# The small x load moved to the head of SyncE's queue in a gated attention and MLP decode kernel

## Chip, core and metric

The kernel runs on one core of one Trainium2 chip. The metric is device microseconds of one execution, as a median over runs: 133.84 us before (three runs, 133.84 to 133.92). Profiles come from one profiled execution; their times are counted from the first instruction.

## What is computed

One token x of 576 numbers goes through two branches that a gate mixes. Branch A is attention of 32 query heads, two for each of 16 key heads, over the last 4096 rows of a cache of 32768. Branch B is a two-layer MLP with 4608 hidden units. All inputs are bf16.

```python
g = sigmoid((x * gate_w).sum(-1))
# branch A, W = 4096, 32 heads of 128, 16 key heads
q = (x @ wq).reshape(1, 1, 32, 128)
k, v = k_cache[:, :, -W:], v_cache[:, :, -W:]      # each repeated for two query heads
a = softmax(q @ k.T * 128**-0.5) @ v @ wo
# branch B
b = gelu(x @ w1 + b1) @ w2 + b2
out = g * a + (1 - g) * b
```

Nearly everything that is read is used once: keys and values of 16 MB each, w_q and w_o of 4.5 MB each and w_1 and w_2 of 5 MB each.

## The kernel before

All big loads are issued by SyncE, one after the other on one queue, into SBUF tiles of 128 partitions. Keys and values come in four groups of four key heads (`load_k`, `load_v`, 4 MB each, L104) into three rotating buffers; w_q, w_1 and w_o share two others (`load_flat`, L126). SyncE waits before a load whose buffer is still being read. The w_2 blocks (L710) come last, into the buffers of keys and values.

The order at the start is written by hand. `load_flat` loads the first half of w_q in two pieces: a plain block of 2048 columns (512 KB, 128 rows of 4096 bytes) and the rest (1.75 MB); between the two it calls `first_keys`, which issues the first group of keys and the small load of x. Then come the second half of w_q, the second keys, the rows of b_1 (L159), x_row and gw_row (L163 and L164, for the gate) and the third keys. Two small loads of b_2 are issued by ScalarE (L139). Each load signals one of eight completion semaphores that are given out in turn, and a load that gets one for the second time waits for the earlier load on it.

`x9` holds x as 64 rows of nine numbers, 18 bytes each. TensorE's order is by hand too: it first transposes head 0 of the keys (L281, eight times four 128x128 matmuls, evicted at L290 by VectorE and at L292 by ScalarE), then spreads x over 128 partitions by one matmul with `dup` (L432), from which VectorE writes `x2` (L440). Heads 1 to 3 are transposed next, and then 36 matmuls give q (L451), which use `x2` and all of w_q. Scores, softmax, values, the first MLP layer and the gate follow while keys and values arrive. At the end w_o and w_2 are multiplied as they land (L752 and L771), and the output is copied (L787) and stored (L788).

Of the kernel before, what the change touches and what calls it, by code (L numbers as in the profile page):

```python
# [16 lines left out]
def kernel(  # L17
# [15 lines left out]
    nc = tc.nc  # L33
# [24 lines left out]
    NM = 9  # L58
# [53 lines left out]
    def load_k(m):  # L112
        return load_kv(A_k_cache, m, "k_t")
# [25 lines left out]
        nc.scalar.dma_start(out=b2_r[0:1, o], in_=B_b2.rearrange("(o n) -> o n", o=1)[:, o])  # L139

    x9 = const.tile([P // 2, NM], BF16, name="x9")

    def first_keys():
        k_tiles[0] = load_k(0)
        nc.sync.dma_start(out=x9[:], in_=A_x.rearrange("a b (i m) -> (a b i) m", m=NM))

    QP = 2 * NM
    wq_t = [  # L150
        load_flat(wq_flat, 0, QP * QC, "wq_t", (NQ * QC,), first_keys),
        load_flat(wq_flat, QP * QC, QP * QC, "wq_t"),
    ]
# [4 lines left out]
    for o in range(2):  # L158
        nc.sync.dma_start(  # L159
            out=b1_r[o : o + 32 * (NQ - 1) + 1 : 32],  # L160
            in_=B_b1.rearrange("(o t k n) -> o t k n", o=2, t=NQ, k=2)[o],
# [17 lines left out]
        out=row_f[:], in_=ident_f[:, 0 : 32 * (NQ - 1) + 1 : 32], axis=AX.X, op=ALU.add  # L179
# [4 lines left out]
        out=dup[:].rearrange("k (i e) -> k i e", e=2),  # L184
        in_=ident[0 : P // 2, 0 : P // 2].rearrange("k (i e) -> k i e", e=1).to_broadcast(
            [P // 2, P // 2, 2]
        ),
    )
    par = const.tile([P, 2], FP32, name="par")
    for o in range(2):  # L190
        nc.vector.tensor_reduce(
            out=par[:, o : o + 1],
            in_=ident_f[:].rearrange("p (i o) -> p o i", o=2)[:, o, :],
# [7 lines left out]
        out=turn[:].rearrange("p j (h q) -> p j h q", h=OJ),  # L201
        in_=ident[:].rearrange("p (o q j) -> p j o q", o=1, j=OJ).to_broadcast(
            [P, OJ, OJ, P // OJ]
        ),
# [4 lines left out]
        out=m_r[:], in_=ident_f[:].rearrange("p (s r) -> p r s", r=R), axis=AX.X, op=ALU.add  # L209
# [4 lines left out]
    for t in range(TB):  # L214
        nc.vector.tensor_reduce(
            out=m_b[:, t, :, :],
            in_=ident_f[:].rearrange("p (g t b q) -> p t g q b", g=HT, t=TB, q=2)[:, t],
# [4 lines left out]
        out=m_b[:].rearrange("p t g q -> p (t g q)"),  # L222
# [5 lines left out]
        out=own[:], in_=ident_f[:].rearrange("p (i g) -> p g i", g=HT), axis=AX.X, op=ALU.add  # L228
# [3 lines left out]
        out=own_r[:].rearrange("p (g q) -> p g q", q=2),  # L232
        in_=own[:].rearrange("p (g o) -> p g o", o=1).to_broadcast([P, HT, 2]),
# [3 lines left out]
        out=perm[:].rearrange("p (g i) -> p g i", g=HT),  # L237
        in_=ident[:].rearrange("p (i g) -> p g i", g=HT),
# [3 lines left out]
        out=pick[:], in_=ident[:].rearrange("p (g x q) -> p x g q", g=HT, q=2)  # L242
# [4 lines left out]
        out=m_c[:], in_=ident_f[:].rearrange("p (t c r) -> p c t r", c=BC, r=R), axis=AX.XY,  # L247
# [4 lines left out]
        out=m_hl[:], in_=ident_f[:].rearrange("p (h q) -> p h q", h=OJ), axis=AX.X, op=ALU.add  # L252
# [10 lines left out]
        out=half[:], in_=ident_f[:].rearrange("p (e c) -> p e c", e=2), axis=AX.X, op=ALU.add  # L263
# [4 lines left out]
    for dst, src in ((sel, ident), (sel_f, ident_f)):  # L268
        nc.vector.tensor_copy(
            out=dst[:].rearrange("p l (o h) -> p l o h", o=2),  # L270
            in_=src[:].rearrange("p (h l x) -> p l x h", h=2, l=2)[:, :, 0:2, :],
# [176 lines left out]
    for b in range(NM * NQ):  # L448
        m, t = b // NQ, b % NQ
# [22 lines left out]
    for l in range(2):  # L472
        nc.vector.tensor_copy(
            out=qz[:].rearrange("p (t l e) n -> p t l e n", l=2, e=2)[:, :, l, :, QZ : QZ + 2],
            in_=qT[:, :, l, :].rearrange("p (e q) t -> p t e q", q=2),
# [228 lines left out]
    for g in range(NG):  # L704
# [10 lines left out]
        out=ot[:], in0=o_sb[:], scalar=g_t[:, 0:1], in1=r_sums[:], op0=ALU.mult, op1=ALU.mult  # L715
# [3 lines left out]
    for j in range(OJ):  # L719
# [3 lines left out]
        out=ow_m[:],  # L723
# [5 lines left out]
    with nc.allow_low_precision("one of the sixteen summands is not zero"):  # L729
        nc.vector.tensor_reduce(  # L730
            out=ow[:].rearrange("p j o -> p (j o)"), in_=ow_m[:], axis=AX.X, op=ALU.add
# [17 lines left out]
    for n, four in enumerate(blocks):  # L749
# [11 lines left out]
        out=part_s[:], in0=b2_r[:].rearrange("p (k n) -> p k n", k=2), scalar=omg[:, 0:1],  # L761
# [57 lines left out]
```

## Time and profile before

| what | value |
|---|---|
| median of the runs | 133.84 us |
| the profiled execution | 133.86 us, of which its span 132.1 us |
| TensorE busy (matmul) | 91.1 us |
| VectorE busy | 62.7 us |
| ScalarE busy | 50.3 us |
| bytes moved, mean rate over the span | 53.79 MB, 407 GB/s |
| granted TensorE clock, mean | 0.859 |

The span runs from the first instruction to the last; what lies around it is in the time of an execution but in no row of the profile. An engine's busy time is a sum over the span and does not say whether it lies in the way of the end. The rows of the queue of SyncE (SPq) are the instructions that issue a transfer; the transfer itself runs later, on 16 DMA engines that work through one ring each in the order of issue.

### The profile page before, as it was taken

To read this page: it belongs to the slowest core of one execution; us is meant where nothing else is said; L and a number is where in the kernel's file an instruction comes from. 1 tells how busy PE (TensorE), PEld (TensorE's weight loads), DVE (VectorE), ACT (ScalarE), POOL (GpSimd) and SP (SyncE) were. 2 spreads that over 40 slices of the span, in tenths; PEclk is the share of its full clock that TensorE was granted. 3 is DMA by queue.
4 is the path that set the end of the run, shared out by engine and by line. 5 is a ranking of instruction groups with operands and counts; after the bars stand their busy time and mean duration, and the time that the engine had idled before them with its cause. 6 is when DMAs were issued, how large, how long until landed. Compare 5 with 4: busy or idle time off the path is not lost.

```text
span 132.1 us, 2606 instructions
## 1 busy us (share of the span) xinstructions
PE 91.1 (69%) x1127; PEld 59.6 (45%) x1127; DVE 62.7 (47%) x138; ACT 50.3 (38%) x89; POOL 2.9 (2%) x10
## 2 busy tenths in 40 slices
PE   0000587986498879487899998994799856294761
PEld 0000585653266646256665575761396421252230
DVE  2940356642256546847545457477376262610021
ACT  3000358870177777483465646670600000000001
POOL 8000000000000000000000000000000000000000
PEclk9999999999999999965579999999985555959555
DMA  4999999999999899999989989998999999999970
GB/s 100 535 397 397 413 445 423 466 471 389 409 476 452 367 447 417 406 458 466 447 371 421 473 372 457 466 432 377 457 466 392 424 396 430 430 427 407 434 272 5
DMA packets 3449, 53.79 MB, mean 407 GB/s; under 512 B 483, under 2 KB 750, under 8 KB 1390
## 3 DMA queue, kind: packets, MB, share of 16 engines
q1 hardware_dynamic: 3434, 53.62, 95.5%
q8 instruction: 9, 0.15, 0.4%
q14 instruction: 2, 0.02, 0.0%
q10 hardware_dynamic: 4, 0.00, 0.0%
HBM read 53.62 MB, written 0.00 MB: 406 GB/s over the span
## 4 chain that ended last, share of the span: by engine, by line
DMA 44%; PE 26%; DVE 14%; issue 6%; ACT 5%; SPq 3%; DVEq 0%; ACTq 0%
DMA w_t<-in_B_w_dram 22%; DMA k_t<-in_A_k_cache_dram 21%; PE tp L281 12%; DVE kT L290 6%; PE s_ps L311 4%; ACT kT L292 3%; PE acc L398 3%; PE h_ps L495 2%; PE pT L367 2%; DVE ez L374 2%; ACT pr L355 2%; PE y_ps L771 1%; SPq L126 1%; DVE h_r L514 1%; DVE mx L331 1%
## 5 line engine op out<-in xcount | busy, mean ns | idle before, releaser
L281 PE MATMUL tp<-perm,k_t 128*128 128x128 bf16 x512 | 44.4, 234 | 20.8 <-DMA k_t<-in_A_k_cache_dram 15.9
L292 ACT CAST kT<-tp 128x512 bf16<-128x512 f32 x80 | 44.0, 587 | 38.8 <-PE tp L281 37.2
L281 PEld LDWEIGHTS <-k_t 128*128 128x128 bf16 x512 | 34.5, 105 | 32.1 <-DMA k_t<-in_A_k_cache_dram 16.4
L290 DVE CAST kT<-tp 128x512 bf16<-128x512 f32 x48 | 32.6, 689 | 34.6 <-PE tp L281 30.6
L311 PE MATMUL s_ps<-kT,qz 128*32 128x512 bf16 x128 | 12.6, 409 | 1.2 <-DVE kT L290 0.9
L398 PE MATMUL acc<-v_t,ez 128*32 128x512 bf16 x128 | 13.0, 507 | 0.0
L787 ACT CAST y<-y_ps 1x144 bf16<-1x144 f32 x2 | 0.5, 270 | 27.3 <-PE y_ps L771 27.3
L374 DVE TENSOR_TENSOR ez<-pT,own_r 128x512 bf16<-128x512 f32 x8 | 5.5, 690 | 3.5 <-PE pT L367 3.3
L752 PE MATMUL part<-w_t,gt 128*1 128x288 bf16 x54 | 4.3, 381 | 3.0 <-DMA w_t<-in_B_w_dram 2.8
L760 DVE SCALAR_TENSOR_TENSOR part_s<-b_r,omg,part 128x576 f32<-128x576 bf16 x1 | 0.8, 815 | 10.7 <-PE part L752 10.7
L355 ACT ACTIVATE pr<-ms,nb 128x2048 bf16<-128x2048 f32 x2 | 4.0, 2002 | 4.6 <-DVE nb L352 4.6
L311 PEld LDWEIGHTS <-qz 128*32 128x32 bf16 x128 | 3.6, 94 | 4.6 <-DVE kT L290 1.2
L367 PE MATMUL pT<-pick,pr 128*128 128x128 bf16 x32 | 4.1, 271 | 2.1 <-ACT pr L355 1.1
L398 PEld LDWEIGHTS <-ez 128*32 128x32 bf16 x128 | 3.4, 114 | 3.7 <-issue 2.7
L367 PEld LDWEIGHTS <-pr 128*128 128x128 bf16 x32 | 3.4, 140 | 3.6 <-ACT pr L355 2.1
L526 PE MATMUL hT<-sel_f,h_r 128*128 128x8 f32 x18 | 4.9, 377 | 0.0
L526 PEld LDWEIGHTS hT<-sel_f,h_r 128*128 128x128 f32 x18 | 4.7, 331 | 0.4 <-DVE nb L352 0.4
L752 PE MATMUL part<-wo_t,ow 128*1 128x288 bf16 x64 | 3.6, 407 | 1.5 <-DVE ow L730 1.5
L414 DVE SCALAR_TENSOR_TENSOR a_s<-acc,m_c,a_s 128x128 f32<-128x128 f32 x12 | 4.2, 351 | 0.4
L421 PEld LDWEIGHTS o_ps<-m_r,a_s 128*128 128x128 f32 x8 | 1.6, 250 | 6.2 <-DVE a_s L414 5.3
L421 PE MATMUL o_ps<-m_r,a_s 128*128 128x8 f32 x8 | 2.0, 319 | 3.2 <-DVE a_s L414 3.1
L752 PEld LDWEIGHTS <-gt 128*1 128x1 bf16 x54 | 1.8, 92 | 5.2 <-issue 4.2
(87 smaller groups left out, 46.3 us busy)
## 6 DMA issues: line engine op xcount, KB each, us to landing
k_t<-in_A_k_cache_dram SPq DMA_DIRECT2D x4, 4096.0 KB, 30.3
v_t<-in_A_v_cache_dram SPq DMA_DIRECT2D x4, 4096.0 KB, 26.0
w_t<-in_B_w_dram SPq DMA_DIRECT2D x2, 2592.0 KB
wo_t<-in_A_wo_dram SPq DMA_DIRECT2D x2, 2304.0 KB, 23.9
w_t<-in_B_w_dram SPq DMA_DIRECT2D x2, 1296.0 KB, 27.3
wq_t<-in_A_wq_dram SPq DMA_DIRECT2D x1, 2304.0 KB
wq_t<-in_A_wq_dram SPq DMA_DIRECT2D x1, 1792.0 KB, 16.0
w_t<-in_B_w_dram SPq DMA_DIRECT2D x1, 864.0 KB
```

The costliest lines, as they stand in the source:

```text
L281: nc.tensor.matmul(tp[:, c * P : (c + 1) * P], lhsT=k_tiles[h // UT][:, (h % UT) * NCH + i * BC + c, :], rhs=perm[:], start=True, stop=True,)
L290: nc.vector.tensor_copy(out=dst, in_=tp[:])
L292: nc.scalar.copy(out=dst, in_=tp[:])
L311: nc.tensor.matmul(s_tiles[t // TB][32 * g : 32 * (g + 1), :, :], lhsT=qz[:, HT * t + g, lo : lo + 32], rhs=kT_v[:, s * CB : (s + 1) * CB, ...
L355: nc.scalar.activation(out=pr[:].rearrange("p c i g -> p (c i) g"), in_=ms[:].rearrange("p c (i g) -> p (c i) g", g=1).to_broadcast([P, CB ...
L367: nc.tensor.matmul(pT[:, c, :, :].rearrange("p x r -> p (x r)"), lhsT=pr[:, n * BC + c, :, :].rearrange("p i g -> p (i g)"), rhs=pick[:].r ...
L374: nc.vector.tensor_tensor(out=ez[:, :, :, n, :, :].rearrange("p t b c r -> p c (t b) r"), in0=pT[:], in1=own_r[:].rearrange("p (a b r) -> ...
L398: nc.tensor.matmul(acc[t][32 * ct : 32 * ct + BC * R, :, :], lhsT=ez[:, t % TB, n // NN, n % NN, :, :].rearrange("p c r -> p (c r)"), rhs= ...
L414: nc.vector.scalar_tensor_tensor(out=a_s[:], in0=acc[t][:, c, :], scalar=m_c[:, c : c + 1], in1=a_s[:], op0=ALU.mult, op1=ALU.add,)
L421: nc.tensor.matmul(o_ps[:], lhsT=a_s[:], rhs=m_r[:], start=True, stop=True)
L526: nc.tensor.matmul(box[0][:, j, :, :].rearrange("p e g -> p (e g)"), lhsT=rows[:, j : j + RJ * (P - 1) + 1 : RJ], rhs=sel_f[:].rearrange(" ...
L752: nc.tensor.matmul(part[32 * t : 32 * t + 1, k, 0:DB], lhsT=col, rhs=w[:, i * D + k * DB : i * D + (k + 1) * DB], start=(n == 0), stop=(n ...
```

## The change

The one instruction that loads `x9` is taken out of `first_keys` and stands right behind the allocation of its tile, so that it is issued before `load_flat` is called for the first time. Shape, source and destination stay as they are.

```diff
     x9 = const.tile([P // 2, NM], BF16, name="x9")
+    nc.sync.dma_start(out=x9[:], in_=A_x.rearrange("a b (i m) -> (a b i) m", m=NM))
 
     def first_keys():
         k_tiles[0] = load_k(0)
-        nc.sync.dma_start(out=x9[:], in_=A_x.rearrange("a b (i m) -> (a b i) m", m=NM))
```

SyncE's first transfers are then x, the plain block of w_q, the first keys and the rest of w_q; before, they were the block, the keys, x and the rest. The instructions of the other engines keep their order. The completion semaphores are given out in the order of the program, so the loads at the start get other ones than before.

## The prediction

> **What bounds the kernel now.** I read the slices of the page first, then the table by stretches, then SyncE's own timeline, then the place where x is used.
>
> The page's slices, whose DMA row is the mean busy share of the 16 DMA engines:
>
> ```profile
> span 132.1 us, 2606 instructions
> ...
> PE 91.1 (69%) x1127; PEld 59.6 (45%) x1127; DVE 62.7 (47%) x138; ACT 50.3 (38%) x89; POOL 2.9 (2%) x10
> ...
> DMA  4999999999999899999989989998999999999970
> ```
>
> No engine is near full, while DMA is at 9 tenths from the second slice almost to the end. The table by stretches says how full (columns: from:to and length, busy us and instructions of PE, PEld, DVE, ACT and POOL, granted clock, DMA share, GB/s):
>
> ```profile
> 1.70:2.70 1.00, 0.00 (x0) 0.00 (x0) 0.34 (x1) 0.57 (x1) 0.93 (x4) 1.00 0.94 127
> 2.70:3.60 0.90, 0.00 (x0) 0.00 (x0) 0.87 (x2) 0.71 (x1) 0.79 (x2) 1.00 1.01 391
> 3.60:13.50 9.90, 0.00 (x0) 0.00 (x0) 4.59 (x18) 0.00 (x0) 0.00 (x0) 1.00 1.02 439
> 13.50:128.00 114.50, 89.77 (x1093) 58.57 (x1097) 56.31 (x116) 48.49 (x86) 0.00 (x0) 0.86 1.00 427
> ```
>
> The share is 0.94 to 1.02 in every stretch from 1.70 to 128.0 us, and from 3.6 us on the rate is 427 to 439 GB/s. So the 53.6 MB of loads are one unbroken stream, and the kernel's time is: when the stream starts, plus its bytes over its rate, plus the tail behind its last packet. The waits of SyncE for PE in the middle (57.1 us in all at L104) cost nothing as long as the ring still holds work. The DMA packet records of the trace give the ends of the stream: first packet at 1.76 us, last w_2 packet at 128.53. PE's last matmuls end at 129.35 and the output is issued at 130.04. The first stretch is the odd one: busy at 0.94, but at 127 GB/s. Of w_q's 128 packets of 4096 bytes the first on each engine took 0.69 us on average (0.16 to 1.19), the usual one 0.159; summed, the excess is 0.69 us per engine.
>
> SyncE's queue at the start (start us, duration us):
>
> ```profile
> 0.73 0.39 SPq L126 DMA_DIRECT2D wq_t<-in_A_wq_dram  x1
> 1.19 0.62 SPq L104 DMA_DIRECT2D k_t<-in_A_k_cache_dram  x1
> 1.86 0.58 SPq L145 DMA_DIRECT2D x<-in_A_x_dram  x1
> 2.48 1.12 SPq L126 DMA_DIRECT2D wq_t<-in_A_wq_dram  x2
> 3.65 0.56 SPq L104 DMA_DIRECT2D k_t<-in_A_k_cache_dram  x1
> 4.56 1.22 SPq L159 DMA_DIRECT2D b_r<-in_B_b_dram  x2
> 7.90 0.30 SPq L163 DMA_DIRECT2D x_row<-in_A_x_dram  x1
> 14.15 0.27 SPq L164 DMA_DIRECT2D gw_row<-in_gate_w_dram  x1
> 14.47 0.60 SPq L104 DMA_DIRECT2D k_t<-in_A_k_cache_dram  x1
> ```
>
> Only the first of these issues is uncovered: the stream starts 1.03 us after w_q's issue begins. Everything behind it is issued while w_q's block and the 4 MB of keys run (to 14.15 us).
>
> And the use of x:
>
> ```profile
> 14.18 1.82 PEld L281 LDWEIGHTS <-k_t 128*128 128x128 bf16 x17 [14.18 <-DMA k_t<-in_A_k_cache_dram]
> ...
> 18.74 0.18 PE L432 MATMUL x_ps<-x,dup 64*128 64x9 bf16 x1
> ```
>
> x was issued at 1.86 and landed 12.5 us later (the page's list of DMA issues), at 14.4 us. Its matmul stands behind the eight transposes of head 0 and ran at 18.74: x was 4.3 us early.
>
> **The change part by part.**
>
> *An earlier x: worth nothing.* PE's order is the same, so L432 still follows head 0's transposes, which wait for the keys; x had 4.3 us to spare.
>
> *The issue leaves its place behind the keys: nothing gained.* There its 0.58 us lay under the transfer of the block and the keys. The remaining w_q is issued 0.6 us earlier relative to the keys, but its packets queue behind the keys' until 13.3 us.
>
> *The issue stands first: the block of w_q, with the whole stream, comes later by it.* Nothing covers it, since no DMA runs before 1.76 us. The trace has no x issue in first place. Below: 0.27 us (gw_row, a small transfer issued after a wait). Above: 0.58 (x's own, behind another issue). I take 0.39, the issue that stands first now, with as clean a queue. The pause to the next issue is 0.04 to 0.07 in the rows above; I take 0.06.
>
> *w_q's issue becomes a second issue.* First in line it took 0.39; the second one now takes 0.62. If the packets follow the end of an issue, up to 0.23 us is added; if they follow its beginning, none. I take 0.10.
>
> *The small packets leave the middle of the stream: a gain.* x is 64 packets of 18 bytes, four on each engine, seen at 13.30 to 13.85 us, 9 ns each with 6 ns between: 4 x 15 ns = 0.06 us off each engine.
>
> *The completion semaphores rotate.* The loads share eight in turn, and the built program shows the waits shift by one: the first b_1 row waits for x in place of w_q's block, the second for the block in place of b_2, x_row and gw_row for the two b_2 halves, and the third keys (L104 at 14.47) for the first keys in place of x. In all, gw_row leaves 6 us sooner and the third keys are released at the keys' landing, as now to 0.3 us. Behind the waiting instructions on SyncE stand only loads whose packets come after the second keys', at 33 us or later. Cost: nothing, covered by the 18 us of w_q and keys queued ahead; it would cost only if that ring ran dry.
>
> *The slow first packets.* The unknown: does x now pay them, or does w_q's block pay them again? By the excess of 0.69 us this can take back the whole shift or add as much. I take it as unchanged: the block still opens 128 rows of w_q for the first time, as it does now. Both ends stay in the range.
>
> Sum: 0.39 + 0.06 + 0.10 - 0.06 = +0.49 us; from 0.27 + 0.06 + 0 - 0.06 = 0.27 to 0.58 + 0.06 + 0.23 - 0.06 = 0.81 without the first packets. Does such a shift reach the end? The stream has no hole to swallow it (share 1.00 from 13.5 to 128.0), and PE, which frees buffers for later loads, gets its keys later by the same amount. The tail of 3.6 us hangs on the last packet and moves along. The profiled execution took 133.86 us: 132.1 of span and 1.76 around it, which stay. It is 0.02 above the median of 133.84. Span 132.1 + 0.5 = 132.6; time 133.84 + 0.49 = 134.33, forecast 134.3.
>
> A rule that speaks against it: the Trainium skill, "DMA: Bandwidth & Descriptors", section "Issuing engines are not separate DMA queues", says of the sequencer's time to initiate a DMA that it "is usually small relative to the DMA itself". By that rule the sum would be about 0 and the time 133.8; it holds for the rows in mid-stream, where 0.5 to 0.6 us of issue lies under 10 us of keys, and no run here yet shows the uncovered case.
>
> **The rivals.**
>
> *Absorbed (not slower).* The slow first packets belong to the engines' start, whatever is moved. Then x's first packets take them: they start at 1.89 on average and end at 1.89 + 0.69 = 2.58, three more follow by 2.63, and w_q's block, ready from 1.89 + 0.55 = 2.44, runs eight packets at 0.165: finished at 3.95. Now its packets give way to the keys' at 3.86 on average. Shift 3.95 - 3.86 - 0.06 = +0.03 us: 133.9. If 18 bytes pay less than 4096 do, the block starts at 2.44, ends at 3.76, and the shift is -0.16: 133.7. It decides if x's excess reaches some 0.4 us. For it: no later first touch of a tensor is slow (the keys' first packets took 1.21 us, as all of theirs). Against it: later packets have the one before to hide behind, so that doesn't prove it; and one first packet took 0.16, which an engine's own start should not allow. The rule of the Trainium skill above, that an issue is small, would give the same total and shares this case's chance.
>
> *Paid twice (slower still).* The delay belongs to the addresses: x's first packets pay it until 2.58 and w_q's pay it again behind them. The block ends at 2.63 + 0.69 + 1.32 = 4.64 instead of 3.86: +0.72 after the 0.06, 134.6. For it: nothing but 16 rows far apart being read at once. Against it: x is 1152 contiguous bytes, and reads of the next packet may already run.
>
> *Swallowed later.* Some wait in the middle is not paced by the stream, and the shift ends there: 133.8. For it: SyncE waits for PE four times at L104. Against it: no stretch has a DMA share under 0.94, so the ring never ran dry at those waits.
>
> **How the numbers follow.** Shifted by the issue: 0.52. Absorbed: 0.27. Paid twice: 0.13. Swallowed or anything else: 0.08. What can't be told from no change is 0.2%, 0.27 us. The forecast's own low end touches that bound, so about a tenth of its chance counts as no change: slower 0.47 + 0.13 + a little of the rest = 0.62. Absorbed with 0.20 of its chance inside the bound, the tenth, and most of the rest: same 0.29. Faster 0.09: the absorbed case beyond its low end of -0.16. The range goes from below the absorbed case's low end, 133.65, to the paid-twice case, 134.65; the likeliest case alone spans 134.1 to 134.6.
>
> **What would show it.** SyncE's first issue is x at about 0.73, w_q's begins near 1.2 instead of 0.73, the keys' near 1.8. The first keys land near 14.6 in place of 14.15, the stream's last packet comes near 129.0 in place of 128.5, and the stretch 13.5 to 128 keeps its share of 1.00. Absorbed would show as w_q's packets at 0.159 us from the first on, and the keys landing at 14.2. Paid twice would show as a slow second beginning, and keys at 14.9. The forecast is wrong if the keys land later but the output doesn't, or if a stretch in the middle shows a share below 0.98.

## The result, and the profile after

The changed kernel takes 134.92 us (median of 7 runs, 134.59 to 135.74) against 133.84 before (7 runs, 133.79 to 134.21): a ratio of 1.0069, 95% interval 1.0048 to 1.0090, or +0.6 to +1.2 us. Measured again, with more runs, it was 134.79 against 133.98, ratio 1.0058 (1.0033 to 1.0084). The forecast of 134.3 had the direction; the time lies above its range. Some runs were disturbed, seven of twelve in one of the experiments below; ratios leave these out, so where a median and a ratio disagree the ratio counts.

The profiled execution took 135.74 us, the slowest of the seven, with a span of 133.9. The page's slices:

```profile
span 133.9 us, 2606 instructions
...
DMA  2999899998999999999989998999999999999940
```

The first digit, 4 before, is 2, and the row then stays as full as it was. The table by stretches, with the columns and stretches shown of before:

```profile
1.70:2.70 1.00, 0.00 (x0) 0.00 (x0) 0.34 (x1) 0.57 (x1) 0.93 (x4) 1.00 0.24 26
2.70:3.60 0.90, 0.00 (x0) 0.00 (x0) 0.88 (x2) 0.71 (x1) 0.80 (x2) 1.00 0.87 141
3.60:13.50 9.90, 0.00 (x0) 0.00 (x0) 4.59 (x18) 0.00 (x0) 0.00 (x0) 1.00 1.07 458
13.50:128.00 114.50, 90.93 (x1083) 59.63 (x1083) 55.52 (x115) 48.50 (x86) 0.00 (x0) 0.82 1.00 426
```

From 1.70 to 2.70 us the share fell from 0.94 to 0.24, and the next stretch moves 141 GB/s instead of 391. From 3.6 us on the shares are as full as before (1.07 and 1.00). The start of SyncE's queue says why (start us, duration us):

```profile
0.73 0.58 SPq L142 DMA_DIRECT2D x<-in_A_x_dram  x1
...
1.36 0.58 SPq L126 DMA_DIRECT2D wq_t<-in_A_wq_dram  x1
...
2.00 0.58 SPq L104 DMA_DIRECT2D k_t<-in_A_k_cache_dram  x1
...
5.75 0.45 SPq L163 DMA_DIRECT2D x_row<-in_A_x_dram  x1
...
6.25 0.28 SPq L164 DMA_DIRECT2D gw_row<-in_gate_w_dram  x1
...
15.39 0.60 SPq L104 DMA_DIRECT2D k_t<-in_A_k_cache_dram  x1
15.42 1.82 PEld L281 LDWEIGHTS <-k_t 128*128 128x128 bf16 x17 [15.42 <-DMA k_t<-in_A_k_cache_dram]
...
19.98 0.18 PE L432 MATMUL x_ps<-x,dup 64*128 64x9 bf16 x1
```

x's issue took 0.58 us though nothing stood before it, and w_q's then 0.58 instead of 0.39. w_q's issue ended at 1.94 in place of 1.12, and its first packet came at 2.56 in place of 1.76 (packet records): 0.62 us after the end of the issue, 0.64 before. x's own 64 packets ran at 2.08 to 2.30, at most 9 ns each. gw_row left at 6.25 instead of 14.15, as the rotated semaphores had it, and nothing was gained by that. x still waits for its turn behind the keys, at 19.98.

The end: the first of the last small w_2 packets came 0.72 us later (127.16 against 126.44), the last packet of the stream 1.82 later (130.35 against 128.53). In this profile the fastest DMA engine is thus late by about the shift and the slowest by 1.1 us more.

### The profile page after: what moved, and what is told of

Same layout as the page of the kernel before. It is cut to its first block, busy times and chain, and to the rows that moved or that the text cites. A ratio compares the mean times of both kernels' runs of the same rounds, so it can differ in the third digit from the quotient of the medians.

```text
span 133.9 us, 2606 instructions
## 1 busy us (share of the span) xinstructions
PE 93.1 (70%) x1127; PEld 60.9 (46%) x1127; DVE 62.7 (47%) x138; ACT 50.3 (38%) x89; POOL 2.9 (2%) x10
## 4 chain that ended last, share of the span: by engine, by line
DMA 45%; PE 27%; DVE 14%; issue 5%; ACT 3%; SPq 3%; DVEq 0%; ACTq 0%
DMA w_t<-in_B_w_dram 23%; DMA k_t<-in_A_k_cache_dram 22%; PE tp L281 12%; DVE kT L290 6%; PE s_ps L311 4%; ACT kT L292 3%; PE acc L398 3%; PE h_ps L495 2%; PE pT L367 2%; DVE ez L374 2%; PE y_ps L771 1%; SPq L126 1%; DVE h_r L514 1%; DVE mx L331 1%; DVE ms L330 1%
## 5 line engine op out<-in xcount | busy, mean ns | idle before, releaser
L281 PE MATMUL tp<-perm,k_t 128*128 128x128 bf16 x512 | 45.0, 235 | 20.9 <-DMA k_t<-in_A_k_cache_dram 16.2
L752 PE MATMUL part<-w_t,gt 128*1 128x288 bf16 x54 | 5.0, 431 | 3.1 <-DMA w_t<-in_B_w_dram 2.9
L367 PE MATMUL pT<-pick,pr 128*128 128x128 bf16 x32 | 4.7, 302 | 1.4 <-DVE ez L374 1.1
L752 PEld LDWEIGHTS <-ow 128*1 128x1 bf16 x64 | 2.1, 119 | 3.0 <-DVE ow L730 1.6
```

The source lines that it names most:

```text
L281: nc.tensor.matmul(tp[:, c * P : (c + 1) * P], lhsT=k_tiles[h // UT][:, (h % UT) * NCH + i * BC + c, :], rhs=perm[:], start=True, stop=True,)
L367: nc.tensor.matmul(pT[:, c, :, :].rearrange("p x r -> p (x r)"), lhsT=pr[:, n * BC + c, :, :].rearrange("p i g -> p (i g)"), rhs=pick[:].r ...
L752: nc.tensor.matmul(part[32 * t : 32 * t + 1, k, 0:DB], lhsT=col, rhs=w[:, i * D + k * DB : i * D + (k + 1) * DB], start=(n == 0), stop=(n ...
```

## Experiments

**The changed kernel again.** No edit.

> The changed kernel once more, for a second profile. Theory I (the uncovered issue delays the whole stream): w_q's first packet again near 2.56 us instead of 1.76, the fastest DMA engine's last packet again +0.72 us, time +0.75 us or a little more, 134.6 to 134.9. Theory E (one engine fell behind by chance at the head, a key packet of 2.04 us, and it alone makes the rest of the +1.08): this profile shows no such packet, or on another load, and its span is nearer to 132.9 than to 133.9. If the 2.04 us packet belongs to the order (theory O), it is there again at 4.5 us and the span is near 133.9.

Measured: 134.79 us, profiled execution 134.84, span 133.0. Its table by stretches:

```profile
1.70:2.70 1.00, 0.00 (x0) 0.00 (x0) 0.34 (x1) 0.57 (x1) 0.93 (x4) 1.00 0.30 22
2.70:3.60 0.90, 0.00 (x0) 0.00 (x0) 0.88 (x2) 0.71 (x1) 0.80 (x2) 1.00 0.72 159
```

The late beginning recurs: first w_q packet at 2.59. The late end does not: the last packet stands at 129.40, +0.87, and no key packet took 2.04 us (in the first profile one at 4.5 us did, and that engine was through with the keys some 0.5 us behind the next one). At the same place four packets took 1.25 to 1.44 us in place of 1.21. So 0.8 us belongs to the change (by the ratio +0.78, interval 0.44 to 1.13); most of the first profile's other 1.0 does not recur.

One figure was not as expected: the fastest engine is late by 0.47 us here, not by 0.72 again. It is late by 0.43 even in the next experiment, where the stream starts on time, so one engine is a poor measure. The mean start of the 256 last small w_2 packets, which takes in all engines, comes +0.83 and +0.64 us later in the two profiles of the changed kernel, and +0.24 in the next experiment.

The first profile also has the lowest granted TensorE clock of its seven runs, 0.827. The clock does not sort the times, though: three of the repeated runs at 0.845 took 134.76, 135.06 and 135.89 us.

**x first, but on ScalarE's queue.** The edit is made in the changed kernel.

```diff
+    x9 = const.tile([P // 2, NM], BF16, name="x9")
+    nc.scalar.dma_start(out=x9[:], in_=A_x.rearrange("a b (i m) -> (a b i) m", m=NM))
     for o in (slice(0, D // 2), slice(D // 2, D)):
...
-    x9 = const.tile([P // 2, NM], BF16, name="x9")
-    nc.sync.dma_start(out=x9[:], in_=A_x.rearrange("a b (i m) -> (a b i) m", m=NM))
```

> x is issued first on ScalarE's queue, at about 0.73 us, beside w_q's block on SyncE. Theory I (SyncE's own issue time): w_q's first packet at 1.76, time 133.8 to 133.9. Rival T (x's 64 small packets at the head, or the making of their descriptors, hold the DMA engines whoever issues them): w_q's first packet at 2.2 us or later and 134.3 or more.

Measured: ratio 1.0007 (0.9983 to 1.0030); 134.09 us against 133.98. The two queues in its timeline:

```profile
0.73 0.38 SPq L126 DMA_DIRECT2D wq_t<-in_A_wq_dram  x1
0.74 0.54 ACTq L139 DMA_DIRECT2D x<-in_A_x_dram  x1
1.18 0.61 SPq L104 DMA_DIRECT2D k_t<-in_A_k_cache_dram  x1
```

x is issued as early as in the changed kernel and for nearly as long, and w_q's first packet is at 1.75 us. So it is SyncE's time that costs: the same issue on another engine, beside w_q's, delays nothing. x's packets are no longer ahead of w_q's here (they ran at 3.53 to 4.14 us, behind the block), so that they cost nothing at the head is read from the changed kernel: there they were through at 2.31, and w_q's first packet came 0.62 us after the end of its own issue, as without them. The rotated semaphores are no cause either: gw_row left at 7.93 us here instead of 14.15. The Trainium skill, "DMA: Bandwidth & Descriptors", section "Issuing engines are not separate DMA queues", says that issuing from several engines saves only the sequencer's issue time; this run agrees, with 0.84 us at the first packet and 0.7 us of time against the changed kernel.

**Other loads first.** The dose is varied: gw_row (six rows of 192 bytes) in x's place, with x back behind the keys; a copy of x in 16 rows of 72 bytes that nothing reads; x and gw_row together.

```diff
+    nc.sync.dma_start(out=gw_row[:], in_=gate_w.rearrange("(r n) -> r n", r=GR))
...
-    nc.sync.dma_start(out=gw_row[:], in_=gate_w.rearrange("(r n) -> r n", r=GR))
```

> x stays behind the keys; another small load, gw_row (6 rows of 192 bytes, issue 0.27 us against x's 0.58), is SyncE's first. Theory I: the stream shifts by 0.27 + 0.05 + up to 0.19 = 0.32 to 0.51 us, time 134.2 to 134.35. Rival F (any first load that isn't the block costs the same, as a fixed start): 134.6 to 134.9. Rival T (the 64 rows of x): no shift, 133.85.

```diff
+    x16 = const.tile([16, D // 16], BF16, name="x16")
+    nc.sync.dma_start(out=x16[:], in_=A_x.rearrange("a b (i m) -> (a b i) m", i=16))
```

> x stays behind the keys; a second copy of the same 1152 bytes in 16 rows of 72 bytes, which nothing reads, is SyncE's first load and uses all 16 DMA engines with one row each (x: 64 rows of 18 bytes, four each; gw_row: six rows of 192). If the issue's 0.58 us and the 0.19 behind it follow the number of rows, it costs about as gw_row: issue 0.35 to 0.42, w_q's first packet at 2.1 to 2.25, 134.2 to 134.4. If they follow the 16 engines or the odd row length, as x: issue near 0.58, first packet at 2.5 to 2.6, 134.7 to 134.9.

```diff
+    nc.sync.dma_start(out=x9[:], in_=A_x.rearrange("a b (i m) -> (a b i) m", m=NM))
+    nc.sync.dma_start(out=gw_row[:], in_=gate_w.rearrange("(r n) -> r n", r=GR))
...
-        nc.sync.dma_start(out=x9[:], in_=A_x.rearrange("a b (i m) -> (a b i) m", m=NM))
...
-    nc.sync.dma_start(out=gw_row[:], in_=gate_w.rearrange("(r n) -> r n", r=GR))
```

> x and then gw_row stand first, ahead of w_q's block. Theory I adds the two shifts: x's 0.80 us and gw_row's 0.39 put w_q's first packet at 1.76 + 0.80 + 0.39 = 2.95 us and the time at 134.0 + 0.8 + 0.3 = 135.1, 134.9 to 135.3. Rival F (one fixed start, paid once whatever stands first): first packet at 2.56, 134.8 as with x alone.

SyncE's first issues with gw_row first:

```profile
0.73 0.37 SPq L142 DMA_DIRECT2D gw_row<-in_gate_w_dram  x1
1.16 0.37 SPq L126 DMA_DIRECT2D wq_t<-in_A_wq_dram  x1
```

with 16 rows first:

```profile
0.73 0.40 SPq L143 DMA_DIRECT2D x<-in_A_x_dram  x1
1.19 0.41 SPq L126 DMA_DIRECT2D wq_t<-in_A_wq_dram  x1
```

and with both first:

```profile
0.73 0.58 SPq L142 DMA_DIRECT2D x<-in_A_x_dram  x1
1.37 0.51 SPq L143 DMA_DIRECT2D gw_row<-in_gate_w_dram  x1
```

| first on the queue | first w_q packet, us | shift | medians, difference | ratio and interval |
|---|---|---|---|---|
| w_q (before) | 1.76 | | | |
| w_q, x on ScalarE | 1.75 | 0 | +0.11 | 1.0007 (0.9983 to 1.0030) |
| gw_row | 2.15 | 0.39 | +0.29 | 1.0012 (0.9988 to 1.0036) |
| 16 rows of x | 2.24 | 0.48 | +0.49 | 1.0040 (1.0024 to 1.0057) |
| x (the change, again) | 2.59 | 0.83 | +0.81 | 1.0058 (1.0033 to 1.0084) |
| x and gw_row | 2.92 | 1.16 | +1.23 | 1.0100 (1.0071 to 1.0130) |

The time grows with the shift, and each interval holds its own shift, so one to one fits. The shifts add: 0.80 + 0.39 = 1.19 was expected of both, 1.16 came. No fixed start is paid. gw_row's time alone cannot be told from no change; it stands only as a point of this row. x's 64 rows of 18 bytes are dear twice, by 0.58 us of its own and 0.2 more on the issue behind it (w_q behind x 0.58, behind 16 rows 0.41, behind gw_row 0.37, first 0.39). The 16 rows also use 16 DMA engines (sixteen 4-byte packets follow the sixteen of 72 bytes in the records), so the number of engines isn't it; the count of rows and their length were not told apart. The 16 rows' 134.48 us lies 0.1 above what was expected of a load with few rows.

**x between block and keys.**

```diff
     def first_keys():
+        nc.sync.dma_start(out=x9[:], in_=A_x.rearrange("a b (i m) -> (a b i) m", m=NM))
         k_tiles[0] = load_k(0)
-        nc.sync.dma_start(out=x9[:], in_=A_x.rearrange("a b (i m) -> (a b i) m", m=NM))
```

> x goes between the plain block of w_q and the first keys: same completion semaphores for the third keys and the gate rows as in the changed kernel, but not first in the queue. Theory I: w_q's first packet is back at 1.76 us; the keys' issue is 0.63 us later but the block's packets cover it; time 133.8 to 133.9, as before. Theory R (the rotation of the semaphores or x ahead of the keys costs the time): 134.6 to 134.9, as in the changed kernel.

Measured: 135.68, ratio 1.0115 (1.0082 to 1.0149), worse than the change itself. Both theories missed. Its start and one stretch:

```profile
0.73 0.40 SPq L126 DMA_DIRECT2D wq_t<-in_A_wq_dram  x1
1.19 0.56 SPq L144 DMA_DIRECT2D x<-in_A_x_dram  x1
1.80 0.58 SPq L104 DMA_DIRECT2D k_t<-in_A_k_cache_dram  x1
...
3.60:5.60 2.00, 0.00 (x0) 0.00 (x0) 1.99 (x5) 0.00 (x0) 0.00 (x0) 1.00 0.92 300
```

The same stretch of the kernel before:

```profile
3.60:5.60 2.00, 0.00 (x0) 0.00 (x0) 1.99 (x5) 0.00 (x0) 0.00 (x0) 1.00 1.28 547
```

w_q's first packet is back at 1.76, but behind the block the stream has a hole: the keys' first packets on the 16 engines came between 3.59 and 5.40 us (before: 3.58 to 4.15), and many took 1.5 to 2.0 us instead of 1.21. The keys, issued 0.6 us later, were not ready when the block was through. The block covers their issue with little to spare: from the start of the keys' issue to the first engine done with the block it is 2.39 us before and 2.42 in the changed kernel, where both are moved alike, and 1.79 here. With the 16 rows first it was 2.28, and no engine stopped.

**A larger block as cover, and a control.** The cut of w_q's first half is moved from 2048 to 6144 columns, once with x between block and keys (the edit above as well) and once with x behind the keys (this edit alone).

```diff
-        load_flat(wq_flat, 0, QP * QC, "wq_t", (NQ * QC,), first_keys),
+        load_flat(wq_flat, 0, QP * QC, "wq_t", (3 * NQ * QC,), first_keys),
```

> x between block and keys as in the run x_second, but the block is three times as large (6144 columns, 12288 bytes a row, 3.8 us of transfer instead of 1.3). Theory L (x_second lost its 1.7 us because the block no longer covers the keys' lead once x's issue stands before it): the hole between 3.6 and 5.6 us is gone and the time is within 0.3 us of the run block3. Rival S (x's 18-byte packets ahead of the keys on each ring slow the keys down, whatever covers them): a hole or long key packets behind x's packets again, at 6 to 8 us, and about 1.5 us over block3.

> The control for x_second_block3: the kernel before with the larger block, x behind the keys. The keys land 2.5 us later but the stream is the same: 133.8 to 134.2 by both theories, if the later start of the transposes has room; up to 2.5 us more if it has not.

Two stretches with x between and the larger block:

```profile
3.60:5.60 2.00, 0.00 (x0) 0.00 (x0) 1.99 (x5) 0.00 (x0) 0.00 (x0) 1.00 1.00 424
5.60:13.50 7.90, 0.00 (x0) 0.00 (x0) 2.60 (x14) 0.00 (x0) 0.00 (x0) 1.00 1.07 458
```

(A packet counts where it starts, so a stretch in which key packets begin can show a share over 1; 1.00 is a full one.) The hole is gone: x's packets ran at 5.89 to 6.64 us and the keys' first ones right behind at 5.92 to 6.65, one of them with 1.28 us, the rest with 1.21. With cover, x ahead of the keys costs the stream nothing. The times don't settle it: they were to lie within 0.3 us of each other, and the ratios are 0.7 us apart, 1.0060 (1.0024 to 1.0095) against 1.0005 (0.9970 to 1.0039) for the control; the intervals overlap, and the runs of both scatter, 133.9 to 136.8 and 133.8 to 137.2, where those of before lie within 1.4 us. Theory L rests here on the trace alone.

**gw_row between block and keys.**

```diff
     def first_keys():
+        nc.sync.dma_start(out=gw_row[:], in_=gate_w.rearrange("(r n) -> r n", r=GR))
         k_tiles[0] = load_k(0)
...
-    nc.sync.dma_start(out=gw_row[:], in_=gate_w.rearrange("(r n) -> r n", r=GR))
```

> gw_row (6 rows, issue 0.37 us) in place of x between the small block and the keys; x stays behind the keys. Theory L alone (only the delay of the keys' issue counts, 0.42 us instead of 0.61): a smaller hole between 3.6 and 5.6 us, 134.3 to 135.0. Rival S (x's 64 rows make the lead longer by themselves): next to no hole, 133.9 to 134.2.

Measured: 136.38, ratio 1.0172 (1.0142 to 1.0201), the worst of all, and outside both expectations. Its issues and the same stretch:

```profile
1.20 0.35 SPq L144 DMA_DIRECT2D gw_row<-in_gate_w_dram  x1
1.60 0.62 SPq L104 DMA_DIRECT2D k_t<-in_A_k_cache_dram  x1
...
3.60:5.60 2.00, 0.00 (x0) 0.00 (x0) 1.99 (x5) 0.00 (x0) 0.00 (x0) 1.00 1.20 433
```

The keys' issue began at 1.60, 2.02 us ahead of the need; the keys' first packets came between 3.62 and 5.12, and seventeen key packets up to 7.7 us took 1.5 to 2.1 us. So x's many rows are not the reason, and a lead of 2.0 us is too short where 2.3 was enough. That 0.4 us cost more here than 0.6 did with x speaks against a simple count. Summed over the packet records, hole and long key packets make 1.5 us per engine in this kernel and 1.4 with x. The last small w_2 packets start 1.48 us later on average in both, which fits; but the last packet of all comes 2.3 us later here (130.84) and 2.2 with x (130.75). So the rest of the 2.4 us stands at the engines that end last, and why they fall behind stays open.

**The keys first.** No block; keys, x, and w_q's first half whole.

```diff
+    first_keys()
     QP = 2 * NM
     wq_t = [
-        load_flat(wq_flat, 0, QP * QC, "wq_t", (NQ * QC,), first_keys),
+        load_flat(wq_flat, 0, QP * QC, "wq_t"),
```

> No plain block of w_q: the first keys are SyncE's first transfer, then x, then w_q's first half whole. Theory L (a load of keys needs far longer than a block of w_q from its issue to its first packets: with x between them they came 1.8 to 3.6 us after the keys' issue began, a block's 1.0 us): the first packet stands at 2.5 to 3.5 us instead of 1.76 and the time is 134.5 to 135.5. Rival A (the slow first packets belong to w_q's rows of 4096 bytes; the keys have packets of 32768): first packet near 2.0, no slow ones, 133.4 to 133.8.

Measured: 135.79, ratio 1.0114 (1.0081 to 1.0147). SyncE's first issue and two stretches:

```profile
0.73 0.63 SPq L104 DMA_DIRECT2D k_t<-in_A_k_cache_dram  x1
...
1.70:2.70 1.00, 0.00 (x0) 0.00 (x0) 0.34 (x1) 0.55 (x1) 0.93 (x4) 1.00 1.91 524
2.70:3.60 0.90, 0.00 (x0) 0.00 (x0) 0.87 (x2) 0.74 (x1) 0.79 (x2) 1.00 0.00 0
```

The first key packets start at 2.15 us, 1.42 after the issue began, and all sixteen take 1.69 to 2.21 us; none starts in the second stretch, as the engines still hold the first. Both expectations fall: the keys start earlier than theory L had it, and rival A's fast packets don't exist. The slow first packets come with engines that had nothing to do, not with w_q's rows: they cost the keys 0.7 us each (1.91 on average against 1.21), as they cost w_q's block 0.69 per engine. A late start of 0.4 us does not make 1.8; the rest was not traced.

## Why the prediction was wrong

Its mechanism was right: the issue that stands first on SyncE is uncovered, the whole stream moves by it, and nothing in the middle swallows it. Its size was not.

- *"The issue stands first"* was mis-sized: 0.39 us was taken, the duration of w_q's issue in that place, and 0.58 was measured. x's own row, written down as the upper bound, was the right one: x takes 0.58 in both places. (Not every load keeps its duration: gw_row takes 0.27 at 14.15 us, 0.37 as the first and 0.51 behind x.) Missing: 0.19.
- *"w_q's issue becomes a second issue"*: 0.10 was taken, 0.19 measured, and the packets follow the end of an issue, so all of it counts. The reason given (second in line) is wrong too: behind gw_row w_q's issue takes 0.37. Missing: 0.09.
- The pause (0.05 instead of 0.06) holds. The packets taken out of the middle were worth half of what was put down: four of them start 6 ns apart on an engine and last 9 ns each, so with the 4-byte packet behind them they fill 0.03 us (13.296 to 13.326), not 0.06. With the measured terms the sum is 0.58 + 0.05 + 0.19 - 0.03 = 0.79; the repeated comparison gives +0.81 by the medians and +0.78 by the ratio.
- *The slow first packets* were taken as unchanged. That was nearly right: w_q's block pays 0.62 and 0.55 us per engine in the two profiles (0.69 before, and 0.60 with x on ScalarE, where nothing runs ahead of it), x's packets 9 ns. Absorbed and paid twice, 40% of the chance between them, fall with it.
- *Swallowed* falls: the last small packets start 0.83 and 0.64 us later on average, and the time moved with them. *An earlier x is worth nothing*, *the issue leaves its place* and *the semaphores rotate* held: L432 stands behind head 0 as ever.
- One sign misleads: the keys were to be there near 14.6 us, or 14.9 if paid twice. TensorE began on them at 15.42 and 15.06 (14.18 before). The keys are there when the slowest engine is, and in the first profile that one had the packet of 2.04 us; w_q's packets show that nothing was paid twice.
- The range ended at 134.65 and held neither 134.79 nor 134.92: its top was the shift at its largest (133.84 + 0.81), with nothing for the engine that happens to end last or for the kernel before, which took 133.98 in the repeat. The first profile's span is 0.9 us over the second's, with one key packet of 2.04 us at the head and a slowest engine 1.1 us further behind than the fastest is late. How often that happens was not settled, and the difference between +0.81 and +1.08 lies within both intervals.

The Trainium skill's sentence ("DMA: Bandwidth & Descriptors", section "Issuing engines are not separate DMA queues"), that a sequencer's time for a DMA is usually small beside the DMA, was weighed against the forecast; here x's issue took 0.58 us and its packets 0.22, w_q's first byte came 0.8 us later, and the measurement decides.

## What to carry to other kernels

When a kernel is one unbroken stream of loads, the issue that stands first is paid in full, about one to one, as with each of the small loads tried here. Put a load there that is quick to issue, and the small ones behind the large loads that cover them, or on another engine's queue, where x cost nothing that the runs show (1.0007). Price a moved issue by the duration of that same load, not by that of the instruction whose place it takes, allow a tenth or two of a us for what stands ahead of it, and count what the next issue loses behind it. A load placed between a short first block and a large load needs the same care, since the cover of the large one may be nearly used up already.

## What was not expected of the hardware

Behind w_q's block of 512 KB the 4 MB of keys followed without a break where their issue began 2.28 to 2.42 us before the first engine was through with the block; with 1.79 and 2.02 us the engines broke off. That is no fixed lead of this load: on idle engines, in the run with the keys first, all sixteen first packets came 1.42 to 1.67 us after the issue began. Why the keys come later behind a block was not settled.

w_q's block needs 1.03 us from the beginning of its issue to its first packet. On that block the Trainium skill ("DMA: Bandwidth & Descriptors", section "Latency and other measured facts") names about 600 ns to the first byte; that agrees with the 0.62 to 0.64 us seen behind the end of the issue.

In the kernel before the lead is 2.39 us, so there is little room for another issue between the block and the keys: x and gw_row there each cost more than x first. First packets on idle engines cost each engine 0.45 to 0.7 us more than the later ones, for w_q's rows in all runs and for the keys where they are first, and x's 18-byte packets ahead of them don't take that over.
